# One user at a time for a PSUM bank in the list that orders a three-layer kernel

## The chip, the cores and the metric

The kernel runs on one core of a Trainium2 chip. The metric is the device time of one execution in microseconds (us), the median of three runs. TensorE (PE) multiplies and writes to PSUM, which has eight banks of 512 words per partition. VectorE (DVE) and ScalarE (ACT) read PSUM and SBUF, GpSimd (POOL) works in SBUF, SyncE (SP) issues DMAs.

## The reference

Three layers follow each other; `N` is 2304 tokens, `D` 512.

```
attention, 4 x 8 heads, 576 positions, head size 64: scores under a window mask
    (32 back, or 128 back in steps of 4), softmax, times v
x  = rows of the attention's output, normed by their root mean square, times rms_g
x  = (silu(x @ w_gate) * (x @ w_val)) @ w_out                    # d_ff = 1536
P  = exp(x @ w_gate2 - max); 8 times: rows, then columns of P scaled to sums
out = sum over 8 experts e of P[:, e] * (relu(x @ w1[e]) @ w2[e])  # F = 1024 each
```

## The kernel before

**Precision.** Each fp32 operand is split into an upper part in a rounded format and the remainder; a product takes three passes (upper by upper, upper by lower, lower by upper, `PASSES`). Every tensor that goes into a product is therefore made twice: a copy (`upper`, mostly ScalarE) and a subtraction (`lower`, VectorE or GpSimd).

**Stages.** Up to about 566 us the attention of 20 tiles and the gated layer run, in six blocks of 384 tokens, while the layer's weights are converted and sums of the experts' weights are prepared in DRAM. Then the experts run: three groups of 768 tokens, and in each 16 halves of an expert, so 48 units. A unit `u` is a first block product (`gemm1_ops`, L1123) and a second (`gemm2_ops`, L1283), each done by a scheme with seven products instead of eight (`STEPS`, L1089). The second of unit `u-1` is interleaved with the first of unit `u`. In group 0 the second weights are split on the core and stored; in groups 1 and 2 they are loaded split.

**Banks.** The seven steps of a unit accumulate in three chains, `CHAIN = "acababa"`: chain a holds steps 0, 2, 4 and 6, b steps 3 and 5, c step 1. In the first product a step is two products `q` of six matmuls with 384 columns, one bank each. In the second a step is three products `jj` of six matmuls with 256 columns: `jj` 0 and 1 share a bank, `jj` 2 has one alone (`jj // 2`, L1304). After each step VectorE adds each `jj`, scaled by `P`, to the output in SBUF (`acc`, L1395). The first product's banks are read by ScalarE and VectorE: `copied` (L1212), `added` (L1222), the two parts of h (`halves_of`, L1133, lines 1140 to 1151), `kept` (L1225), and after step 6 the four steps of L1245 and L1121. One tile of two banks (`pair`) serves chain a of even units and chains c and b of odd units; the other chains take single banks from a pool of six.

**The list.** Nothing runs by a loop on the chip. Each operation is an `Op` (L84): engine, a cost, what it reads and writes (keys), which slot it takes and frees. `Plan.add` (L106) makes dependences from the keys: a reader waits for the last writer, a writer for the readers as well; two readers of one key don't wait for each other. `Plan.run` (L122) plays the operations through a model of the engines: at each moment, each free engine starts the ready operation of the lowest rank. The order of the starts is the order in which instructions are emitted, so each engine's queue is fixed by it. Ranks of the first stages are by name (`RANK`, L34), and which engine takes a piece is in `PICK` (L64); those of the units are `at(u, s) = 1000 + 14 u + 2 s` (L1097), plus 1 for the second product. Semaphores are put in afterwards by the layer below, from the tiles and banks that instructions really touch, not from the keys. So the list sets the order on each engine, and where its idea of a wait is wrong, an engine stands at an instruction that the list thought ready.

**Keys before.** A bank's key of the first product is `("bank", u, chain, q)`; the parts of h and `kept` read it. In the second product the key is `("y", u, chain, jj)`, so the two `jj` of one bank are independent in the list. Weights of unit `u+1` are split at rank `at(u + 1, j) - 6`, behind gates on products of unit `u` (L1717, L1730).

Of the kernel before, what the change touches and what calls it, by code (L numbers as in the profile page):

```python
# [19 lines left out]
P = 128  # L20
# [50 lines left out]
    "lower c2o": "DVE", "scaled 0": "ACT", "scaled 1": "ACT", "scaled 10": "ACT", "scaled 11": "DVE",  # L71
    "scaled 12": "ACT", "scaled 2": "ACT", "scaled 6": "DVE", "scaled 7": "DVE", "scaled 8": "DVE",
# [11 lines left out]
class Op:  # L84

    def __init__(self, eng, cost, emit, reads=(), writes=(), take=(), free=(), table=None, size=0, pick=None,
                 beside=None):
        self.beside = beside
        if pick:
            self.name, self.costs = pick  # L90
            eng = PICK.get(self.name, eng)
            cost = self.costs[eng]
        self.eng, self.cost, self.emit, self.reads, self.writes = eng, cost, emit, reads, writes
        self.take, self.free, self.table, self.size = take, free, table, size
        self.rank, self.after, self.end, self.got = None, [], None, None


class Plan:

    HOP, EXTRA, LOAD, LATENCY, RATE, BESIDE = 0.1, 0.08, 1.3, 2.0, 360.0, 1.35  # L100

    def __init__(self, slots):
        self.ops, self.slots = [], {tag: list(names) for tag, names in slots.items()}
        self.writer, self.readers = {}, {}
# [17 lines left out]
    def run(self):  # L122
# [12 lines left out]
        while len(order) < len(self.ops):  # L135
# [12 lines left out]
            for i, (_, o) in enumerate(ready):  # L148
                if free[o.eng] > now or o.take and not any(self.slots[tag] for tag in o.take):
                    continue  # L150
                if o.take:
                    tag = next(tag for tag in o.take if self.slots[tag])
                    o.got = (tag, self.slots[tag].pop(0))
                span = o.cost * ((o.beside or self.BESIDE) if o.eng == "DVE" and free.get("POOL", 0.0) > now else 1.0)
                if o.table and o.table != table:
                    span, table = span + self.LOAD, o.table
                free[o.eng] = now + span if span else now + 0.01
                heappush(events, free[o.eng])
                if o.size:
                    link = max(link, now + span) + o.size / self.RATE  # L160
                    o.end = link + self.LATENCY
                else:
                    o.end = now + span + self.EXTRA
                for owner in o.free:
                    heappush(back, (o.end + self.HOP, len(order), owner.got if isinstance(owner, Op) else owner))
                    heappush(events, o.end + self.HOP)
                order.append((now, o))
                started.append(i)
                for u in users[o]:
                    needs[u] -= 1  # L170
                    if not needs[u]:
                        at = max(d.end + (0.0 if d.eng == u.eng else self.HOP) for d in u.after)
                        heappush(coming, (at, place[u], u))
                        heappush(events, at)
            for i in reversed(started):
                del ready[i]
        for _, o in order:
            o.emit()
# [4 lines left out]
def attention_moe_kernel(  # L183
# [81 lines left out]
    def att_ops(n, blk, c0, bufs, wide=False, last=(), held=()):  # L265
# [169 lines left out]
        for h in range(2):  # L435
            @op("ACT", 0.33, [("XT", n)], [("hi", n, h)])
# [4 lines left out]
            @op("DVE", 0.4, [("XT", n), ("hi", n, h), ("lo", n, 0)], [("lo", n, h)], free=[back] if h else [])  # L441
# [681 lines left out]
    def gemm1_ops(u):  # L1123
# [9 lines left out]
        def halves_of(s, m, q, key, src, relu, eng):  # L1133
            x = {}

# [8 lines left out]
            def lower():  # L1144
# [9 lines left out]
                "ACT", 0.41, upper, [key] + ([("hu", u, m, 0)] if q else []), [("hu", u, m, q)],  # L1154
                take=("xn", "h", "h2") if q == 0 else (),
            )
            if q == 0:
                h_owner[u, m] = x["up"]
            x["lo"] = Op(
                eng, 0.475, lower, [key, ("hu", u, m, q)], [("hh", u, m, q)],  # L1160
# [3 lines left out]
            add(s, x["up"])  # L1164
            return add(s, x["lo"])
# [663 lines left out]
```

## Time and profile before

| | us |
|---|---|
| median of 3 runs (2214.47 to 2222.55) | 2215.64 |
| the profiled execution, own time | 2215.74 |
| its span, first to last instruction | 2213.7 |
| TensorE busy | 2052.2 |
| TensorE granted clock, mean share of full | 0.98 |

In the profile, "idle before" is what an engine stood before an instruction, and the releaser named with it is what ended the wait. `ya`, `yb`, `yc` are the banks of the second product's chains, `pa`, `pb`, `pc` those of the first; `p`, `pq`, `u`, `r` are copies in SBUF; `h_a` and `h_s` are parts of h, `w_a`, `w_s`, `w_t`, `w_b` split weights. "x6" is six matmuls merged to one row.

### The profile page before, as it was taken

To read this page: it belongs to the slowest core of one execution; us is meant where nothing else is said; L and a number is where in the kernel's file an instruction comes from. 1 tells how busy PE (TensorE), PEld (TensorE's weight loads), DVE (VectorE), ACT (ScalarE), POOL (GpSimd) and SP (SyncE) were. 2 spreads that over 40 slices of the span, in tenths; PEclk is the share of its full clock that TensorE was granted. 3 is DMA by queue.
4 is the path that set the end of the run, shared out by engine and by line. 5 is a ranking of instruction groups with operands and counts; after the bars stand their busy time and mean duration, and the time that the engine had idled before them with its cause. 6 is when DMAs were issued, how large, how long until landed. Compare 5 with 4: busy or idle time off the path is not lost.

```text
span 2213.7 us, 40898 instructions
## 1 busy us (share of the span) xinstructions
PE 2052.2 (93%) x15654; PEld 1987.2 (90%) x15654; DVE 1456.0 (66%) x2906; ACT 1093.4 (49%) x2298; POOL 1047.6 (47%) x975
## 2 busy tenths in 40 slices
PE   6999999999899999989999989899899999999998
PEld 5999999999888888988998988899899899999998
DVE  7886545453686878768656666666665666666665
ACT  7744524332556556556554444444445544444442
POOL 1311454561466767567654443444444444435441
PEclk9999999999999999999999999999999999999999
DMA  7513788884555777777875555665576554554561
GB/s 282 185 51 109 260 277 277 280 273 157 186 211 210 263 278 257 252 260 253 316 259 187 184 181 160 201 212 186 176 254 218 167 199 161 167 180 157 184 191 47
DMA packets 210164, 459.84 MB, mean 208 GB/s; under 512 B 16560, under 2 KB 59440, under 8 KB 209968
## 3 DMA queue, kind: packets, MB, share of 16 engines
q1 hardware_dynamic: 209072, 456.44, 60.8%
q8 instruction: 123, 2.02, 0.4%
q10 hardware_dynamic: 896, 0.79, 0.1%
q14 instruction: 73, 0.60, 0.1%
HBM read 344.44 MB, written 112.72 MB: 207 GB/s over the span
## 4 chain that ended last, share of the span: by engine, by line
PE 59%; DVE 21%; DMA 7%; ACT 7%; POOL 3%; issue 3%; SPq 0%; DVEq 0%; ACTq 0%; POOLq 0%
PE pa L1183 12%; PE ya L1308 12%; PE pb L1183 8%; PE yb L1308 5%; PE pc L1183 4%; PE pg L707 4%; DVE acc L1395 4%; PE pv L707 4%; PE po L631 4%; PE yc L1308 3%; DMA spare<-in_w 3%; DVE h_a L1147 2%; DVE pq L1121 2%; ACT h_s L1142 2%; DVE p L1121 2%
## 5 line engine op out<-in xcount | busy, mean ns | idle before, releaser
L1395 DVE SCALAR_TENSOR_TENSOR acc<-ya,Pm,acc 128x256 f32<-128x256 f32 x510 | 242.0, 478 | 147.5 <-PE ya L1308 142.8
L1007 POOL TENSOR_TENSOR w_s<-w0s,w_s 128x512 fp32r<-128x512 f32 x192 | 253.9, 1327 | 168.8 <-ACT w_s L1003 168.4
L1007 POOL TENSOR_TENSOR w_a<-w0r,w_a 128x512 fp32r<-128x512 f32 x144 | 187.5, 1307 | 196.5 <-ACT w_a L1003 193.9
L1308 PE MATMUL ya<-w_t,h_s 128*128 128x256 f32 x1728 | 256.4, 284 | 17.6 <-DVE acc L1395 16.9
L1308 PEld LDWEIGHTS ya<-w_t,h_s 128*128 128x128 f32 x1728 | 236.9, 191 | 23.5 <-DVE acc L1395 20.4
L1151 POOL TENSOR_TENSOR h_s<-r,h_s 128x384 fp32r<-128x384 f32 x96 | 102.8, 1072 | 326.7 <-ACT h_s L1142 279.2
L1183 PE MATMUL pa<-x_t,w_s 128*128 128x384 f32 x1152 | 238.5, 342 | 2.4 <-ACT pq L1212 1.8
L1183 PEld LDWEIGHTS pa<-x_t,w_s 128*128 128x128 f32 x1152 | 194.8, 190 | 5.8 <-ACT pq L1212 2.0
L1308 PE MATMUL ya<-w_b,h_a 128*128 128x256 f32 x864 | 138.9, 300 | 46.1 <-DVE acc L1395 46.1
L1308 PEld LDWEIGHTS ya<-w_b,h_a 128*128 128x128 f32 x864 | 124.3, 203 | 54.5 <-DVE acc L1395 54.1
L707 PE MATMUL pg<-xn,w_g 128*128 128x384 f32 (+2 forms) x912 | 170.4, 335 | 0.0
L707 PE MATMUL pv<-xn,w_v 128*128 128x384 f32 (+2 forms) x912 | 167.5, 331 | 0.0
L631 PE MATMUL po<-h,w_o 128*128 128x384 f32 x864 | 161.1, 339 | 0.4 <-DVE h L738 0.4
L1003 ACT CAST w_s<-w0s 128x512 fp32r<-128x512 f32 x192 | 118.9, 625 | 82.9 <-POOL w_s L1007 35.4
L707 PEld LDWEIGHTS pg<-xn,w_g 128*128 128x128 f32 x912 | 155.8, 191 | 1.0
L707 PEld LDWEIGHTS pv<-xn,w_v 128*128 128x128 f32 x912 | 153.1, 188 | 1.4
L631 PEld LDWEIGHTS po<-h,w_o 128*128 128x128 f32 x864 | 151.8, 190 | 1.5 <-DVE h L738 0.7
L1151 POOL TENSOR_TENSOR h_s<-p,h_s 128x384 fp32r<-128x384 f32 x96 | 110.2, 1148 | 77.7 <-ACT h_s L1142 67.6
L1308 PE MATMUL yb<-w_t,h_a 128*128 128x256 f32 x864 | 128.5, 284 | 15.9 <-DVE acc L1395 12.0
L1183 PE MATMUL pc<-x_b,w_a 128*128 128x384 f32 x576 | 131.6, 368 | 12.1 <-DVE h_s L1151 11.1
L1308 PEld LDWEIGHTS yb<-w_t,h_a 128*128 128x128 f32 x864 | 117.3, 190 | 21.4 <-DVE acc L1395 16.5
L1395 DVE SCALAR_TENSOR_TENSOR acc<-yb,Pm,acc 128x256 f32<-128x256 f32 x258 | 122.8, 477 | 15.3 <-PE yb L1308 15.1
(215 smaller groups left out, 4582.8 us busy)
## 6 DMA issues: line engine op xcount, KB each, us to landing
w_t<-split SPq DMA_DIRECT2D x128, 512.0 KB, 3.6
w0r<-in_w SPq DMA_DIRECT2D x96, 512.0 KB, 5.8
w0s<-sums SPq DMA_DIRECT2D x96, 512.0 KB, 6.0
w_b<-split SPq DMA_DIRECT2D x96, 512.0 KB, 4.5
split<-w_t SPq DMA_DIRECT2D x64, 512.0 KB, 2.8
split<-w_b SPq DMA_DIRECT2D x48, 512.0 KB, 4.5
spare<-in_w SPq DMA_DIRECT2D x42, 512.0 KB, 5.0
sums<-spare SPq DMA_DIRECT2D x42, 512.0 KB, 4.1
```

What stands on the lines that cost most here:

```text
L631: nc.tensor.matmul(x[dc], lhsT=weights["o", f][:, a, dc * P : dc * P + P], rhs=hs[blk, f][:, bb, :n], start=k == 0, stop=k == 11,)
L707: nc.tensor.matmul(ps, lhsT=weights[nm, kt, fg][:, a, fo * P : fo * P + P], rhs=xns[blk][kt // 2][:, kt % 2, bb, c0:c1], start=k == 0, sto ...
L1003: nc.scalar.copy(w1s[u, m][:, :, 0, :], q[m])
L1007: engines[x["lo"].eng].tensor_tensor(out=v[:, :, 1, :], in0=q[m], in1=v[:, :, 0, :].bitcast(F32), op=ALU.subtract)
L1121: nc.vector.scalar_tensor_tensor(out=out, in0=x, scalar=0.0, in1=y, op0=ALU.max, op1=op)
L1142: nc.scalar.copy(hh[u, m][:, q, 0, :], src())
L1147: nc.vector.scalar_tensor_tensor(out=lo, in0=src(), scalar=0.0, in1=hi.bitcast(F32), op0=ALU.max, op1=ALU.subtract)
L1151: engines[x["lo"].eng].tensor_tensor(out=lo, in0=src(), in1=hi.bitcast(F32), op=ALU.subtract)
L1183: nc.tensor.matmul(banks[chain, q], lhsT=w1s[u, a][:, kt, hl, q * P : q * P + P], rhs=xc[g, b, kt][:, xl, :TH], start=fresh and k == 0, st ...
L1308: nc.tensor.matmul(ps, lhsT=hh[u, a][:, q, hl, jj * P : jj * P + P], rhs=w2s[u, b][:, q, wl, :], start=fresh and k == 0 and jj != 1, stop= ...
L1395: nc.vector.scalar_tensor_tensor(out=dst, in0=ps(), scalar=scale(), in1=dst, op0=ALU.mult, op1=ALU.add)
```

## The change

- **Bank keys.** Operations that read a bank of the first product now write its key, so in the list they follow each other (`halves_of`: `alone`; `kept`; two of the last steps), and `kept` is put between the two parts of h. In the attention the two upper parts now come first and the two lower ones write the bank's key.
- **One operation for a shared bank.** `jj` 0 and 1 of a second product are one operation of twelve matmuls with one key; `jj` 2 stays alone.
- **The model's clockwork.** Latency 0.12 and 0.09 us instead of 0.1 and 0.08, 0.2 behind TensorE; an operation that follows one on its own engine starts at its end; slots of single banks (and of h and xn) come back in a queue that is shared, in the order in which they were freed. Products of the routing get 0.8 us of slack.
- **Weights earlier.** Rank `- 12` instead of `- 6`; the gate of the second weights one step earlier for odd `j`.
- **RANK and PICK** are replaced: other ranks for loads, conversions, attention tiles and blocks of the first stages, other engines for some of the pieces (not shown).

```diff
-    HOP, EXTRA, LOAD, LATENCY, RATE, BESIDE = 0.1, 0.08, 1.3, 2.0, 360.0, 1.35
+    HOP, EXTRA, LOAD, LATENCY, RATE, BESIDE = 0.12, 0.09, 1.3, 2.0, 360.0, 1.35
+    PE_EXTRA = 0.2
...
+    def slot(self, o, now):
+
+        for tag in o.take:
+            if self.slots[tag]:
+                queue = self.queues.get(self.shared.get(tag, tag))
+                if queue is None or queue and queue[0] <= now:
+                    return tag
...
-                        at = max(d.end + (0.0 if d.eng == u.eng else self.HOP) for d in u.after)
+                        at = max(d.done if d.eng == u.eng and not d.size else d.end + self.HOP for d in u.after) + u.slack
...
-            @op("ACT", 0.33, [("XT", n)], [("hi", n, h)])
+            @op("ACT", 0.33, [], [("XT", n), ("hi", n, h)])
             def upper(h=h):
...
-            @op("DVE", 0.4, [("XT", n), ("hi", n, h), ("lo", n, 0)], [("lo", n, h)], free=[back] if h else [])
+        for h in range(2):
+            @op("DVE", 0.4, [("hi", n, h)], [("XT", n), ("lo", n, h)], free=[back] if h else [])
             def lower(h=h):
...
+            alone = [key] if key[0] == "bank" else []
...
-                "ACT", 0.41, upper, [key] + ([("hu", u, m, 0)] if q else []), [("hu", u, m, q)],
+                "ACT", 0.41, upper, [key] + ([("hu", u, m, 0)] if q else []), [*alone, ("hu", u, m, q)],
...
-                eng, 0.475, lower, [key, ("hu", u, m, q)], [("hh", u, m, q)],
+                eng, 0.475, lower, [key, ("hu", u, m, q)], [*alone, ("hh", u, m, q)],
...
             add(s, x["up"])
+            if between:
+                add(s, between)
             return add(s, x["lo"])
...
-                    low = halves_of(s, m, q, key, ps, True, "DVE")
-                    keep = add(s, Op("ACT", 0.372, kept, [key], [(tag, u, q)]))
+                    keep = Op("ACT", 0.372, kept, [], [key, (tag, u, q)])
+                    low = halves_of(s, m, q, key, ps, True, "DVE", keep)
...
-            for jj in range(3):
-                key = ("y", u, chain, jj)
+            for y, some in enumerate(((0, 1), (2,))):
+                key = ("y", u, chain, y)
...
-                    "PE", 6 * 0.1203, product, [("hh", u, a, 0), ("hh", u, a, 1), ("w2", u, b)], [key],
-                    take=ANY if fresh and jj != 1 else (), free=[h_owner[u, a]] if jj == 2 else [],
+                    "PE", len(some) * 6 * 0.1203, product, [("hh", u, a, 0), ("hh", u, a, 1), ("w2", u, b)], [key],
+                    take=ANY if fresh else (), free=[h_owner[u, a]] if y else [],
...
             for jj in range(3):
-                key = ("y", u, chain, jj)
+                key = ("y", u, chain, jj // 2)
...
-        })
+        }, {"mm": "b", "o": "b", "single": "b", "xn": "h"}, ("m", "m2"))
...
-                        plan.add(gated(three[:1], u, (3 + j) // 2), at(u + 1, j) - 6)
-                        plan.add(three[1:], at(u + 1, j) - 6)
+                        plan.add(gated(three[:1], u, (2 + j) // 2), at(u + 1, j) - 12)
+                        plan.add(three[1:], at(u + 1, j) - 12)
...
-                    plan.add(gated(ops[2 * j : 2 * j + 1], u, (2 + j) // 2), at(u + 1, j) - 6)
-                    plan.add(ops[2 * j + 1 : 2 * j + 2], at(u + 1, j) - 6)
+                    plan.add(gated(ops[2 * j : 2 * j + 1], u, (2 + j) // 2), at(u + 1, j) - 12)
+                    plan.add(ops[2 * j + 1 : 2 * j + 2], at(u + 1, j) - 12)
```

## Rows read from the trace of the kernel before

**Rows 1.** The page, busy time of each engine.
```profile
PE 2052.2 (93%) x15654; PEld 1987.2 (90%) x15654; DVE 1456.0 (66%) x2906; ACT 1093.4 (49%) x2298; POOL 1047.6 (47%) x975
```

**Rows 2.** Busy time by stretch: stretch, length, PE, PEld, DVE, ACT, POOL; clock, DMA.
```profile
0.00:54.00 54.00, 32.20 (x827) 27.89 (x827) 42.84 (x95) 39.18 (x83) 5.49 (x12) 1.00 0.78 287
...
600.00:1118.00 518.00, 474.46 (x3219) 458.46 (x3218) 394.13 (x767) 312.24 (x659) 347.01 (x280) 0.99 0.73 260
1118.00:2190.00 1072.00, 994.40 (x6657) 968.12 (x6656) 680.25 (x1368) 503.74 (x1068) 476.19 (x404) 0.97 0.56 184
```

**Rows 3.** Who waited, TensorE, 600 us to the end: total us, times, longest.
```profile
PE ya L1308 <- DVE acc L1395: 63.0, 28, 3.0
PE yb L1308 <- DVE acc L1395: 13.1, 16, 2.3
PE pc L1183 <- DVE h_s L1151: 11.1, 7, 1.9
PE pa L1183 <- ACT p L1212: 9.7, 11, 1.7
PE pb L1183 <- DVE u L1239: 8.9, 14, 1.9
```

**Rows 4.** Timeline, one turn of units: start us, us, engine, line, operation [idle before].
```profile
1417.75 0.88 PE L1308 MATMUL ya<-w_b,h_a 128*128 128x256 f32 x6
...
1418.47 0.88 PE L1308 MATMUL yc<-w_b,h_a 128*128 128x256 f32 x6
...
1420.92 0.47 DVE L1395 SCALAR_TENSOR_TENSOR acc<-ya,Pm,acc 128x256 f32<-128x256 f32 x1
...
1421.77 0.47 DVE L1395 SCALAR_TENSOR_TENSOR acc<-ya,Pm,acc 128x256 f32<-128x256 f32 x1
...
1422.30 0.98 PE L1308 MATMUL ya<-w_b,h_a 128*128 128x256 f32 x6 [2.95 <-DVE acc L1395]
```

**Rows 5.** Timeline of TensorE: three of the stalls that come again.
```profile
1213.61 1.65 PE L1308 MATMUL ya<-w_b,h_a 128*128 128x256 f32 x6 [2.96 <-DVE acc L1395]
...
1572.90 0.98 PE L1308 MATMUL ya<-w_t,h_s 128*128 128x256 f32 x6 [2.32 <-DVE acc L1395]
...
2162.02 1.65 PE L1308 MATMUL ya<-w_b,h_a 128*128 128x256 f32 x6 [2.96 <-DVE acc L1395]
```

**Rows 6.** Timeline of TensorE at a steady place: what a product takes.
```profile
1426.86 1.21 PE L1183 MATMUL pa<-x_t,w_s 128*128 128x384 f32 x6
1427.90 0.87 PE L1308 MATMUL yc<-w_b,h_a 128*128 128x256 f32 x6
1428.61 0.69 PE L1183 MATMUL pa<-x_t,w_s 128*128 128x384 f32 x3
```

**Rows 7.** Timeline of ScalarE: the first copy of three units that follow each other.
```profile
1889.08 0.47 ACT L1212 COPY p<-pa 128x384 f32<-128x384 f32 x1
...
1923.53 0.48 ACT L1212 COPY p<-pa 128x384 f32<-128x384 f32 x1 [0.65 <-PE pa L1183]
...
1955.73 0.47 ACT L1212 COPY p<-pa 128x384 f32<-128x384 f32 x1
```

**Rows 8.** Two stretches of 10 us: length, PE busy, granted clock, DMA share, GB/s.
```profile
1140.00:1150.00 10.00, 8.16 (x59) 1.00 0.61 185
...
1960.00:1970.00 10.00, 9.19 (x45) 0.66 0.18 54
```

**Rows 9.** Timeline of TensorE just behind a long stall.
```profile
1894.98 1.92 PE L1183 MATMUL pc<-x_b,w_a 128*128 128x384 f32 x6
1896.70 1.48 PE L1308 MATMUL ya<-w_b,h_a 128*128 128x256 f32 x6
1897.98 1.51 PE L1183 MATMUL pc<-x_b,w_a 128*128 128x384 f32 x6
```

**Rows 10.** Who waited, whole run: the remainder behind the second copy.
```profile
DVE h_a L1147 <- ACT pq L1225: 51.4, 61, 2.1
```

**Rows 11.** The page, the costliest group on VectorE.
```profile
L1395 DVE SCALAR_TENSOR_TENSOR acc<-ya,Pm,acc 128x256 f32<-128x256 f32 x510 | 242.0, 478 | 147.5 <-PE ya L1308 142.8
```

More of the change, by code (lines that the diff above doesn't have):

```diff
@@ L34 @@
 RANK = {
[26 rows of a table removed]
[26 rows of a table added]
 }
 PICK = {
[6 rows of a table removed]
-    "lower c2o": "DVE", "scaled 0": "ACT", "scaled 1": "ACT", "scaled 10": "ACT", "scaled 11": "DVE",
-    "scaled 12": "ACT", "scaled 2": "ACT", "scaled 6": "DVE", "scaled 7": "DVE", "scaled 8": "DVE",
[8 rows of a table removed]
[7 rows of a table added]
+    "scaled 0": "ACT", "scaled 1": "ACT", "scaled 10": "ACT", "scaled 11": "ACT", "scaled 12": "ACT",
+    "scaled 16": "DVE", "scaled 2": "ACT", "scaled 6": "DVE", "scaled 7": "ACT", "scaled 8": "ACT",
+    "split 1": "DVE", "taken 0 0": "DVE", "taken 1 0": "ACT", "upper c0a 0": "ACT", "upper c0a 1": "POOL",
[7 rows of a table added]
 }
@@ L86, in __init__ @@
     def __init__(self, eng, cost, emit, reads=(), writes=(), take=(), free=(), table=None, size=0, pick=None,
-                 beside=None):
-        self.beside = beside
+                 beside=None, slack=0.0):
+        self.beside, self.slack = beside, slack
         if pick:
@@ L94, in __init__ @@
         self.take, self.free, self.table, self.size = take, free, table, size
-        self.rank, self.after, self.end, self.got = None, [], None, None
+        self.rank, self.after, self.end, self.done, self.got = None, [], None, None, None
 class Plan:
-    HOP, EXTRA, LOAD, LATENCY, RATE, BESIDE = 0.1, 0.08, 1.3, 2.0, 360.0, 1.35
-    def __init__(self, slots):
+    HOP, EXTRA, LOAD, LATENCY, RATE, BESIDE = 0.12, 0.09, 1.3, 2.0, 360.0, 1.35
+    PE_EXTRA = 0.2
+    def __init__(self, slots, shared, named):
         self.ops, self.slots = [], {tag: list(names) for tag, names in slots.items()}
+        self.shared, self.named = shared, named
+        self.queues = {}
+        for tag, names in self.slots.items():
+            if tag not in named:
+                pool = shared.get(tag, tag)
+                self.queues[pool] = self.queues.get(pool, []) + [0.0] * len(names)
         self.writer, self.readers = {}, {}
@@ L120, in add, with order @@
             self.ops.append(o)
-    def run(self):
+    def slot(self, o, now):
[4 more added lines that the diff above has]
+                    return tag
+    def order(self):
         place = {o: (RANK.get(o.rank[0], o.rank[0]), o.rank[1]) for o in self.ops}
@@ L148, in run @@
             for i, (_, o) in enumerate(ready):
-                if free[o.eng] > now or o.take and not any(self.slots[tag] for tag in o.take):
+                if free[o.eng] > now:
                     continue
                 if o.take:
-                    tag = next(tag for tag in o.take if self.slots[tag])
+                    tag = self.slot(o, now)
+                    if tag is None:
+                        continue
                     o.got = (tag, self.slots[tag].pop(0))
+                    if tag not in self.named:
+                        self.queues[self.shared.get(tag, tag)].pop(0)
                 span = o.cost * ((o.beside or self.BESIDE) if o.eng == "DVE" and free.get("POOL", 0.0) > now else 1.0)
@@ L156, in run @@
                     span, table = span + self.LOAD, o.table
-                free[o.eng] = now + span if span else now + 0.01
+                free[o.eng] = now + span if span else now + 0.001
                 heappush(events, free[o.eng])
+                o.done = now + span
                 if o.size:
@@ L162, in run @@
                 else:
-                    o.end = now + span + self.EXTRA
+                    extra = 0.0 if o.eng == "NONE" else self.PE_EXTRA if o.eng == "PE" else self.EXTRA
+                    o.end = now + span + extra
                 for owner in o.free:
-                    heappush(back, (o.end + self.HOP, len(order), owner.got if isinstance(owner, Op) else owner))
-                    heappush(events, o.end + self.HOP)
+                    tag, name = owner.got if isinstance(owner, Op) else owner
+                    at = o.end + self.HOP
+                    heappush(back, (at, len(order), (tag, name)))
+                    heappush(events, at)
+                    if tag not in self.named:
+                        self.queues[self.shared.get(tag, tag)].append(at)
                 order.append((now, o))
@@ L176, in run @@
                 del ready[i]
+        return order
+    def run(self):
+        order = self.order()
         for _, o in order:
@@ L1131, in add, with halves_of @@
             return o
-        def halves_of(s, m, q, key, src, relu, eng):
+        def halves_of(s, m, q, key, src, relu, eng, between=None):
             x = {}
+            alone = [key] if key[0] == "bank" else []
             def upper():
@@ L1260, in gemm1_ops @@
                     add(s, Op("ACT", 0.41, clipped, [], [key]))
-                    hold["r", q] = add(s, Op("DVE", 0.465, step_r, [("p1", u, q), key, "right"], [("r", u, q)], take=("r",), beside=1.0))
+                    hold["r", q] = add(s, Op("DVE", 0.465, step_r, [("p1", u, q), "right"], [key, ("r", u, q)], take=("r",), beside=1.0))
                     add(s, Op("DVE", 0.465, step_s1, [("u4", u, q)], [key], free=[hold["u4", q]], beside=1.0))
-                    add(s, Op("DVE", 0.465, step_p1, [key], [("p1", u, q)], beside=1.0))
+                    add(s, Op("DVE", 0.465, step_p1, [], [key, ("p1", u, q)], beside=1.0))
                     add(s, Op("DVE", 0.465, step_pq, [("p1", u, q)], [("pq", u, q)], beside=1.7))
@@ L1297, in gemm2_ops, with product @@
             row, col = ((0, 0), (0, 0), (1, 0), (1, 1), (1, 1), (1, 0), (0, 1))[s]
-            for jj in range(3):
-                key = ("y", u, chain, jj)
-                def product(s=s, a=a, b=b, chain=chain, fresh=fresh, jj=jj):
-                    if fresh and jj != 1:
-                        banks[chain, jj // 2] = bank(f"y{chain}_{u}_{jj // 2}")
-                    ps = banks[chain, jj // 2][:, 256 * (jj % 2) : 256 * (jj % 2) + 256]
-                    k = 0
-                    for q in range(2):
-                        for hl, wl in PASSES:
-                            nc.tensor.matmul(
-                                ps,
-                                lhsT=hh[u, a][:, q, hl, jj * P : jj * P + P],
-                                rhs=w2s[u, b][:, q, wl, :],
-                                start=fresh and k == 0 and jj != 1,
-                                stop=k == 5,
-                                skip_group_check=True,
-                            )
-                            k += 1
+            for y, some in enumerate(((0, 1), (2,))):
+                key = ("y", u, chain, y)
+                def product(s=s, a=a, b=b, chain=chain, fresh=fresh, y=y, some=some):
+                    if fresh:
+                        banks[chain, y] = bank(f"y{chain}_{u}_{y}")
+                    for jj in some:
+                        ps = banks[chain, y][:, 256 * (jj % 2) : 256 * (jj % 2) + 256]
+                        k = 0
+                        for q in range(2):
+                            for hl, wl in PASSES:
+                                nc.tensor.matmul(
+                                    ps,
+                                    lhsT=hh[u, a][:, q, hl, jj * P : jj * P + P],
+                                    rhs=w2s[u, b][:, q, wl, :],
+                                    start=fresh and k == 0 and jj != 1,
+                                    stop=k == 5,
+                                    skip_group_check=True,
+                                )
+                                k += 1
@@ L1318, in gemm2_ops @@
                 o = Op(
-                    "PE", 6 * 0.1203, product, [("hh", u, a, 0), ("hh", u, a, 1), ("w2", u, b)], [key],
-                    take=ANY if fresh and jj != 1 else (), free=[h_owner[u, a]] if jj == 2 else [],
-                )
-                if jj:
-                    o.after.append(products[u, "y", s, jj - 1])
-                if fresh and jj != 1:
-                    hold[chain, jj // 2] = o
-                products[u, "y", s, jj] = add(s, o)
-                if jj == 2:
+                    "PE", len(some) * 6 * 0.1203, product, [("hh", u, a, 0), ("hh", u, a, 1), ("w2", u, b)], [key],
@@ L1328, in gemm2_ops @@
+                    take=ANY if fresh else (), free=[h_owner[u, a]] if y else [],
+                )
+                if y:
+                    o.after.append(products[u, "y", s, 0])
+                if fresh:
+                    hold[chain, y] = o
+                products[u, "y", s, y] = add(s, o)
+                if y:
                     add(s, close([o] + ([stores[u, b]] if (u, b) in stores else []), [w_owner[1, u, b]]))
             for jj in range(3):
-                key = ("y", u, chain, jj)
+                key = ("y", u, chain, jj // 2)
@@ L1421, in put @@
             def put(fn):
-                ops.append(Op(eng, cost, fn, reads, writes, take, free, table))
+                ops.append(Op(eng, cost, fn, reads, writes, take, free, table, slack=0.8 if eng == "PE" else 0.0))
                 return ops[-1]
```

80 rows, old and new, of tables (PICK, RANK) are left out of this document.

## Prediction

> **What bounds the kernel now.** I read the page's busy times first. The reader is to see TensorE at 2052.2 of 2213.7 us [rows 1], 93 per cent, the others at 66 per cent or less: TensorE is the bound, and only what makes it stand or slows it counts. The stretches say where it stands [rows 2]: 21.8 us of the first 54, when weights and attention tiles have only begun to come, little more until 566, then 518.00 - 474.46 = 43.5 us from 600 to 1118 (group 0) and 1072.00 - 994.40 = 77.6 from 1118 to 2190. So 121.1 us of standing lie among the units. In the same two stretches the granted clock is 0.99 and 0.97, which is 0.01 x 518 + 0.03 x 1072 = 37.3 us of clock lost.
>
> The waits name what ended the standing [rows 3]: 63.0 + 13.1 = 76.1 us are a second product that waits for `acc`, the rest are a dozen small causes, all on banks of the first product. The timeline shows one such wait [rows 4]. `ya` of `jj` 0 starts at 1417.75, `yc` at 1418.47, and then TensorE stands 2.95 us until 1422.30, when `ya` of `jj` 1 starts, just behind the `acc` of 1421.77. That `acc` reads `jj` 0. The two halves don't share a word, they share a bank: the semaphores keep them apart, the list of before thought them free of each other, and so put the product where TensorE must stand at it. It comes again: 14 stalls of 2.95 to 2.96 us from 1213 to 2162, one for two units, and six of 2.31 or 2.32, the last at 1572.90 [rows 5]. 14 x 2.96 = 41.4 and 6 x 2.31 = 13.9 leave 20.8 of the 76.1.
>
> The floor comes from rows at a steady place [rows 6]: six matmuls of 384 columns take 1.04 us until the next product starts, six of 256 take 0.71. A unit has 14 and 21 of them: 14 x 1.04 + 21 x 0.71 = 29.5 us, and two units 58.9. Two units take 1955.73 - 1889.08 = 66.65 us [rows 7]; the 7.7 us above the floor are standing and clock.
>
> The clock: in 10 us with 8.16 busy, so 1.84 of standing, it stayed at 1.00; in the 10 us behind a stall of 2.96 it was 0.66, so some time was spent at the lower of the two levels, 1.2 instead of 2.4 GHz [rows 8]. What that costs is in the products behind the stall [rows 9]: 1.92, 1.48 and 1.51 us against 1.21, 0.87 and 1.21 [rows 6], 1.62 us together. 20 stalls of over 2 us times 1.62 are 32.4 of the 37.3.
>
> **The change part by part.** *One operation for `jj` 0 and 1.* No instruction is added or taken away; twelve matmuls stand where six stood. (a) At the 14 stalls TensorE then has `jj` 1 of `ya` and of `yc` to do, 2 x 0.71 = 1.42 us, before it needs another bank. 14 x 1.42 = 19.9 us come back. (b) The other 1.54 us of each I take as half gained, because the list now sees the wait and may put a product of the first kind or an `acc` ahead; 14 x 0.77 = 10.8. Bounds: 0, if VectorE is what is late and all banks are taken, and 21.6. (c) The six stalls of 2.31 are the same pattern at step 2, with other work in hand: 13.9 gone. (d) Of the 20.8 us of other waits for `acc`, two thirds, 13.9; bounds 0 and 20.8. What it costs: the `acc` of `jj` 0 now starts one product later, 0.71 us. It is covered as long as VectorE, busy 680.25 of 1072 us [rows 2], catches up before chain a comes round two steps later; if the cover fails, rival 4 is the price.
>
> The page "PSUM — Partial Sum Buffer" of the Trainium skill, section "PSUM bank collisions raise a hardware error", says that any two of TensorE, ScalarE and VectorE on one bank and the same partitions at once are an error, reads against reads and disjoint columns included, so that they have to be kept apart by bank. The trace agrees with its 2.95 us at 1422.30. Read against this change, the rule says that the wait can't be removed, only turned round: all 7 x 48 pairs of halves now hold their first `acc` back by 0.71 us, 239 us of VectorE's lateness in all, and the time would be 2216 + 239 less the gains if all of it came onto TensorE's path; I count none of it, on VectorE's share.
>
> *Bank keys of the first product.* The remainder of h waits for the copy beside it, a read behind a read, 51.4 us in 61 waits [rows 10], which the list did not know. That moves nothing by itself: the real wait was there. What is gained is that TensorE's order allows for it. 121.1 - 76.1 = 45.0 us of standing are of this kind (`pc` behind `h_s`, `pa` behind `p`, `pb` behind `u`, [rows 3]); (e) I take a third, 15.0, bounds 0 and 45.0, the low side because the longest of them, `pc` behind `h_s`, waits for the pair of banks itself, which the old list knew too. The latencies, the shared queue of slots and the slack of the routing products have the same answer and are in this third.
>
> *Clock.* (f) With no stall over 2 us left most of the loss goes; two thirds of 37.3, 24.9 us. Bounds 0 and 37.3.
>
> *Weights earlier.* The same casts and subtractions, put ahead of other work of ScalarE and GpSimd, and in group 0 the stores on SyncE with them. No wait of TensorE among the units names a weight or a DMA, so being earlier gains nothing. It can cost: a cast ahead of `copied` or `kept` holds a bank longer. The nearest row is `pa` behind `p`, 9.7 us [rows 3]; bounds -9.7 and +9.7, value 0, since a third of it is already in (e).
>
> *RANK and PICK.* The same work in another order until 566 us. There are 21.8 us of standing in the first 54 [rows 2] to win, and an order that starts the dense products later loses as much: bounds -22 and +22, value 0, for nothing in the trace says which.
>
> Sum: 19.9 + 10.8 + 13.9 + 13.9 + 15.0 + 24.9 = 98.4 us. The profiled execution took 2215.74, 0.1 over the median of the runs, so 2215.7 - 98.4 = 2117.3; I say 2117.
>
> **The rivals.** *1, the forecast*, some 40 per cent of the standing left: 2117, own range 2085 to 2150.
>
> *2, nearly all goes.* The list's new idea of a bank is right everywhere and other products fill each hole. 121.1 + 37.3 = 158.4 us; at 85 per cent, 134.6: 2081. For it: the stalls repeat to 0.01 us, so they come from the order alone. Against it: around a turn VectorE gets to the last `acc` of the old unit only at 1420.92 [rows 4], and banks are the limit there.
>
> *3, the stall changes its name.* At the turn VectorE is late, not the order: TensorE does 1.42 us more, then stands for as long at the next fresh bank, because the `acc` come later by as much. Then (a), (b), (e) and (f) are nothing, (c) and (d) stay: 27.8 us, 2188. For it: the `acc` of 1421.77 comes 3 us after its product's end. Against it: VectorE does in that time steps that could come after.
>
> *4, slower.* The doubled product holds the first `acc` back 0.71 us, VectorE's queue at a turn outlasts TensorE's work in hand, and the stall, which now comes at 14 of 47 turns, comes at 16 more. Each costs 2.96 + 1.62 = 4.58 us, 73 in all, less the 27.8 of (c) and (d): 2215.7 + 45.5 = 2261. It decides from the point where VectorE's backlog at a turn exceeds two products of the first and three of the second kind, 2 x 1.04 + 3 x 0.71 = 4.2 us. Against it: an `acc` is 0.48 us [rows 11], three are 1.4, and step 2 comes that much later only in the unit's middle.
>
> *5, the list hardly moves.* Semaphores already kept the banks apart; the order, fixed by ranks, comes out nearly the same, and what the first stages win or lose is under 11 us: 2216.
>
> **How the numbers follow.** Chances: forecast 0.48, rival 2 0.22, rival 3 0.15, rival 4 0.08, rival 5 0.07. The range 2060 to 2205 holds the first three and leaves out rival 4, most of rival 5 and a rest of rival 2 whose first stages win 22 us as well. A measurement of this kernel can tell some 0.5 per cent, 11 us, from no change. Faster by more than that: 0.48 + 0.22 + 0.14 of rival 3 = 0.84. Within it: 0.01 of rival 3 and 0.07 of rival 5, 0.08. Slower: 0.08.
>
> **What would show it.** In the changed kernel's profile the twelve matmuls of `ya` stand as one row, no second product waits for an `acc` of its own bank's other half, and the waits for `acc` fall from 76 to under 30 us. (a) to (c): no stall of TensorE over 2 us after 1200. (e): waits on `pc`, `pa`, `pb` of 30 us. (f): granted clock 0.99 over the span, no 10 us under 0.80 after 1200. Two units take 62 to 63 us in group 2. Rival 3 shows as stalls of 1.5 to 3 us at the turns named `pc` or a fresh `ya`; rival 4 as stalls at odd and even turns. The first stages: the units start at 566 plus or minus 22. I am wrong in the mechanism if the waits for `acc` stay over 50 us, and in the sum if the units start much later than now.

## The result, and the profile after

The changed kernel takes 2124.94 us (median of 4 runs, 2117.82 to 2131.09), the kernel before 2215.05 beside it: ratio 0.9599, interval 0.9537 to 0.9661. The profiled execution after took 2117.82, its span is 2116.0, so 97.7 us are gone from the span. All numbers below are of the profiled executions unless a ratio stands there.

Busy time on the page of the changed kernel, to lay beside [rows 1]:

```profile
PE 2008.1 (95%) x15654; PEld 1970.1 (93%) x15654; DVE 1457.0 (69%) x2892; ACT 1082.1 (51%) x2310; POOL 1041.3 (49%) x975
```

TensorE is still the bound. Its busy time fell by 44.1 us though it does the same 15654 matmuls. Where the 97.7 us came from is told by ScalarE's first copies of units 0, 16, 32 and 47 (start, length), first of the kernel before, then of the changed one:

```profile
570.69 0.47 ACT L1212 COPY p<-pa 128x384 f32<-128x384 f32 x1
...
1110.45 0.48 ACT L1212 COPY p<-pa 128x384 f32<-128x384 f32 x1
...
1658.34 0.48 ACT L1212 COPY p<-pa 128x384 f32<-128x384 f32 x1 [0.65 <-PE pa L1183]
...
2156.93 0.47 ACT L1212 COPY p<-pa 128x384 f32<-128x384 f32 x1
```
```profile
563.36 0.47 ACT L1246 COPY p<-pa 128x384 f32<-128x384 f32 x1
...
1091.75 0.85 ACT L1246 COPY p<-pa 128x384 f32<-128x384 f32 x2
...
1596.08 0.85 ACT L1246 COPY p<-pa 128x384 f32<-128x384 f32 x2
...
2066.73 0.85 ACT L1246 COPY p<-pa 128x384 f32<-128x384 f32 x2
```

The first stages gave 7.3 us, group 0 gave 11.4 (539.8 to 528.4), group 1 43.6 (547.9 to 504.3), group 2 up to its last unit 27.9 (498.6 to 470.7), and the rest 7.5.

The stretches after, as in [rows 2] (length, TensorE busy, granted clock, DMA share, GB/s):

```profile
0.00:54.00 54.00, 29.28 (x853) 1.00 0.76 277
...
600.00:1092.00 492.00, 459.86 (x3128) 0.98 0.73 261
1092.00:2092.00 1000.00, 962.59 (x6674) 0.99 0.62 199
```

The waits of TensorE from 590 on, as in [rows 3] (total, times, longest; five of fifteen rows):

```profile
PE pc L1217 <- DVE h_s L1183: 33.7, 17, 2.1
PE pc L1217 <- DVE acc L1430: 11.0, 18, 1.9
PE yc L1343 <- DVE acc L1430: 8.9, 5, 2.1
PE pb L1217 <- DVE u L1273: 7.4, 6, 2.2
...
PE yb L1343 <- DVE acc L1430: 0.2, 1, 0.2
```

No `ya` waits for VectorE's `acc` any more, and `yb` does for 0.2 us: the two rows that held 76.1 us are gone. In their place `pc`, the new unit's first product in the pair of banks, waits for `h_s`, the last reader of the pair: 33.7 us, before 11.1. All rows together are 73.3 us, before 121.1.

TensorE's timeline at a turn of the changed kernel (start, us; [idle before <-releaser]):

```profile
1869.33 2.25 PE L1217 MATMUL pa<-x_b,w_s 128*128 128x384 f32 x12
1871.41 2.31 PE L1343 MATMUL ya<-w_b,h_s 128*128 128x256 f32 x18
1873.56 2.25 PE L1217 MATMUL pa<-x_b,w_a 128*128 128x384 f32 x12
1875.65 2.31 PE L1343 MATMUL ya<-w_b,h_a 128*128 128x256 f32 x18
1880.00 2.35 PE L1217 MATMUL pc<-x_b,w_a 128*128 128x384 f32 x12 [2.05 <-DVE h_s L1183]
1882.19 2.31 PE L1343 MATMUL yc<-w_b,h_a 128*128 128x256 f32 x18
```

Two things are to be seen. Each row is a whole step: 12 matmuls of the first product, then 18 of the second, where before halves alternated (six and six, [rows 6]). And at 1880.00 TensorE has stood 2.05 us. This comes at every second turn, 16 times from 1124.08 to 2068.44; the turns between have 0.15 to 0.47. VectorE at the same turn shows what the pair waited for:

```profile
1870.38 0.86 DVE L1430 SCALAR_TENSOR_TENSOR acc<-yb,Pm,acc 128x256 f32<-128x256 f32 x2
...
1872.12 0.56 DVE L1152 SCALAR_TENSOR_TENSOR r<-p,pa 128x384 f32<-128x384 f32 x1 [0.87 <-ACT pa L1279]
...
1876.67 1.17 DVE L1152 SCALAR_TENSOR_TENSOR pq<-pq,p 128x384 f32<-128x384 f32 x1
1877.77 1.25 DVE L1430 SCALAR_TENSOR_TENSOR acc<-ya,Pm,acc 128x256 f32<-128x256 f32 x3
1878.94 1.00 DVE L1183 TENSOR_TENSOR h_s<-pa,h_s 128x384 fp32r<-128x384 f32 x2
```

All eight steps of L1152 run first, from 1872.12 to 1877.8, then three `acc`, then the two remainders that free the pair.

### The profile page after: what moved, and what is told of

Read it like the earlier page. It is cut to its first block, busy times and chain, and to the rows that moved or that the text cites. A ratio compares the mean times of both kernels' runs of the same rounds, so it can differ in the third digit from the quotient of the medians.

```text
span 2116.0 us, 40970 instructions
## 1 busy us (share of the span) xinstructions
PE 2008.1 (95%) x15654; PEld 1970.1 (93%) x15654; DVE 1457.0 (69%) x2892; ACT 1082.1 (51%) x2310; POOL 1041.3 (49%) x975
## 4 chain that ended last, share of the span: by engine, by line
PE 67%; DVE 24%; ACT 5%; issue 2%; DMA 1%; POOL 0%; SPq 0%; DVEq 0%; ACTq 0%; POOLq 0%
PE pa L1217 11%; PE ya L1343 9%; PE pb L1217 8%; PE yb L1343 7%; PE pv L738 6%; PE pg L738 6%; PE po L662 6%; PE pc L1217 6%; PE yc L1343 5%; DVE pq L1152 4%; DVE acc L1430 3%; DVE h_a L1179 2%; DVE p L1152 2%; DVE pa L1152 2%; DVE r L1152 2%
## 5 line engine op out<-in xcount | busy, mean ns | idle before, releaser
L1430 DVE SCALAR_TENSOR_TENSOR acc<-ya,Pm,acc 128x256 f32<-128x256 f32 x510 | 216.6, 471 | 46.7 <-PE ya L1343 46.7
L1343 PE MATMUL ya<-w_t,h_s 128*128 128x256 f32 x1728 | 223.2, 283 | 1.3 <-ACT acc L1389 1.2
L1217 PE MATMUL pa<-x_t,w_s 128*128 128x384 f32 x1152 | 218.9, 337 | 4.5 <-ACT pq L1246 2.2
L1343 PEld LDWEIGHTS ya<-w_t,h_s 128*128 128x128 f32 x1728 | 218.8, 191 | 2.2 <-ACT acc L1389 1.5
L1430 DVE SCALAR_TENSOR_TENSOR acc<-yb,Pm,acc 128x256 f32<-128x256 f32 x258 | 111.7, 476 | 106.1 <-PE yb L1343 106.1
L1217 PE MATMUL pc<-x_b,w_a 128*128 128x384 f32 x576 | 125.6, 371 | 46.2 <-DVE h_s L1183 33.7
L1217 PEld LDWEIGHTS pc<-x_b,w_a 128*128 128x128 f32 x576 | 109.7, 208 | 53.7 <-DVE h_s L1183 37.2
L1343 PE MATMUL yc<-w_b,h_a 128*128 128x256 f32 x864 | 118.2, 292 | 12.3 <-DVE acc L1430 8.9
L1343 PEld LDWEIGHTS yc<-w_b,h_a 128*128 128x128 f32 x864 | 115.8, 200 | 13.6 <-ACT h_s L1174 12.6
L991 POOL TENSOR_TENSOR spare<-spare 128x256 f32<-128x256 f32 x126 | 96.8, 771 | 63.4 <-DMA spare<-in_w 35.0
L1172 ACT ACTIVATE h_a<-pc 128x384 fp32r<-128x384 f32 x96 | 47.6, 495 | 144.5 <-DVE pc L1256 140.8
```

The source lines that it names most:

```text
L991: engines[o.eng].tensor_tensor(out=out_, in0=in0, in1=in1, op=alu)
L1172: nc.scalar.activation(hh[u, m][:, q, 0, :], src(), AF.Relu)
L1217: nc.tensor.matmul(banks[chain, q], lhsT=w1s[u, a][:, kt, hl, q * P : q * P + P], rhs=xc[g, b, kt][:, xl, :TH], start=fresh and k == 0, st ...
L1343: nc.tensor.matmul(ps, lhsT=hh[u, a][:, q, hl, jj * P : jj * P + P], rhs=w2s[u, b][:, q, wl, :], start=fresh and k == 0 and jj != 1, stop= ...
L1430: nc.vector.scalar_tensor_tensor(out=dst, in0=ps(), scalar=scale(), in1=dst, op0=ALU.mult, op1=ALU.add)
```

## The experiments

Each ran in three rounds beside the kernel before; a ratio is to that kernel. Of each edit only the main lines are shown. Line numbers of an experiment may differ by a few from those above.

**a1, the merge alone** (kernel before, with `jj` 0 and 1 as one operation and one key):

```diff
-            for jj in range(3):
-                key = ("y", u, chain, jj)
+            for y, some in enumerate(((0, 1), (2,))):
+                key = ("y", u, chain, y)
```

> The kernel before with one part of the change alone: jj 0 and 1 of a second product are one operation with one key. Theory 1 (the stall between the halves of a bank is what the change removed): 2125 to 2150 us, waits of TensorE for acc under 30 us. Theory 2 (the rule that an operation starts right at the end of its predecessor on the same engine regroups TensorE's order into whole steps, and that alone does it): more than half of the 90 us stays away, 2175 or more. Theory 3 (the first stages' new ranks are most of it): 2205 or more.

2124.89 us, 0.9601 (0.9572 to 0.963): all of the change's gain. The waits of `ya` and `yb` for `acc` (here L1396) fall from 76.1 to 2.7 us. What stands is the first product's, in halves of a step:

```profile
PE pb L1183 <- DVE h_a L1147: 17.7, 11, 1.8
PE pc L1183 <- DVE h_a L1147: 15.5, 18, 0.9
PE pc L1183 <- DVE h_s L1151: 14.1, 21, 1.2
```

All its waits are 77.7 us (73.3 in the change). So the other waits rose here too, from 45.0 to 75.0: of the 73 us that the cure took from one wait, 30 came back under other names.

**a2, the rule alone** (kernel before, with only the model's rule for an operation behind one of its own engine; three separate `jj` and their three keys stay):

```diff
-  at = max(d.end + (0.0 if d.eng == u.eng else self.HOP) for d in u.after)
+  at = max(d.done if d.eng == u.eng and not d.size else d.end + self.HOP for d in u.after)
```

> The kernel before with the rule for operations on the same engine alone (start at the end of the predecessor, not 0.08 us behind it). Theory 1: 2190 or more, the stalls at jj 1 stay. Theory 2: 2120 to 2150, the three jj stand together in TensorE's order, two units take 62 to 64 us in group 2. Theory 3: 2205 or more.

2110.03 us, 0.9538 (0.9511 to 0.9564). The first theory fell: one line of the model removes the stall without the merge, and no `ya` or `yb` waits for VectorE's `acc`. The second theory's order came, its time was better than its range. By the code of the list, with the old rule the next `jj` became ready 0.08 us behind the end of the one before, so at that moment the list found only the other product ready and took it; with the new one the next `jj` is ready at once, has the lowest rank and follows. TensorE then runs in whole steps, and the two `jj` of a bank stand together anyway. The price is the wait of the pair, here as a total and at one turn:

```profile
PE pc L1184 <- DVE h_s L1152: 40.5, 23, 5.8
...
1868.52 2.35 PE L1184 MATMUL pc<-x_b,w_a 128*128 128x384 f32 x12 [2.04 <-DVE h_s L1152]
```

**a3, the change without the merge:**

```diff
-            for y, some in enumerate(((0, 1), (2,))):
-                key = ("y", u, chain, y)
+            for jj in range(3):
+                key = ("y", u, chain, jj)
```

> The changed kernel with jj 0, 1 and 2 as three operations with three keys again. Theory 1: 2170 or more, stalls of 2 to 3 us behind acc come back. Theory 2: 2117 to 2140.

2107.49 us, 0.9521 (0.9489 to 0.9553), with the same whole steps and the same 33.7 us of `pc` behind `h_s`. Beside the rule the merge is not needed. It may even cost: the waits of `pc` and `yc` for `acc` (here L1429, in the change L1430) are 4.4 us here and 19.9 in the change, most of them in group 0, and all waits are 67.9 and 73.3. The times differ by some 17 us, but the two intervals touch, so by time the two can't be told apart. The time is below theory 2's range as well.

**a4, the change with the old rule:**

```diff
-  at = max(d.done if d.eng == u.eng and not d.size else d.end + self.HOP for d in u.after) + u.slack
+  at = max(d.end + (0.0 if d.eng == u.eng else self.HOP) for d in u.after) + u.slack
```

> The changed kernel with the old rule for operations on the same engine (0.09 us behind TensorE's others, 0.2 behind TensorE itself). Theory 1: 2117 to 2140, since the merge is there. Theory 2: 2150 or more, single products interleaved again and small bubbles between them.

2089.38 us, 0.9444 (0.9414 to 0.9473), faster than the change and clear of its interval, some 34 us. The halves came back as theory 2 said, but both theories' times were too long. This is the version that beats both kernels. Its three longest waits:

```profile
PE pb L1217 <- ACT h_a L1172: 12.4, 17, 1.0
PE pc L1217 <- DVE h_s L1183: 11.5, 21, 0.7
PE pa L1217 <- ACT p L1246: 7.9, 8, 1.3
```

The same stretch of both (busy of PE, PEld, DVE, ACT, POOL; clock), first of a4, then of the change:

```profile
1092.00:2037.00 945.00, 924.00 (x6455) 914.13 (x6454) 636.02 (x1323) 487.12 (x1042) 465.85 (x398) 1.00 0.63 207
```
```profile
1092.00:2037.00 945.00, 909.64 (x6303) 902.43 (x6304) 639.04 (x1299) 472.99 (x1023) 449.70 (x392) 0.99 0.64 204
```

a4 stands 21.0 of 945 us at clock 1.00, the change 35.4 at 0.99. The same turn in a4, TensorE and VectorE, shows how it goes:

```profile
1846.46 1.21 PE L1217 MATMUL pa<-x_b,w_s 128*128 128x384 f32 x6
...
1850.70 0.48 DVE L1430 SCALAR_TENSOR_TENSOR acc<-ya,Pm,acc 128x256 f32<-128x256 f32 x1
...
1851.55 0.48 DVE L1430 SCALAR_TENSOR_TENSOR acc<-ya,Pm,acc 128x256 f32<-128x256 f32 x1
...
1853.22 0.48 DVE L1430 SCALAR_TENSOR_TENSOR acc<-ya,Pm,acc 128x256 f32<-128x256 f32 x1
...
1854.96 1.60 PE L1343 MATMUL yc<-w_b,h_a 128*128 128x256 f32 x12
...
1857.14 1.31 PE L1217 MATMUL pc<-x_b,w_a 128*128 128x384 f32 x6 [0.58 <-DVE h_s L1183]
```

From step 6's first product to the pair's release it takes 10.68 us here (1846.46 to 1857.14) and 10.67 in the change (1869.33 to 1880.00): the pair is not free earlier. But VectorE puts the old unit's `acc` between its steps, a single bank is free by 1854.96, and TensorE does twelve matmuls of `yc` there; it then stands 0.58 us and not 2.05. That this makes the whole gain is argued from this turn, not shown.

**b2, the first product's keys alone** (kernel before with `halves_of`, `kept` and the last steps of the change):

```diff
-  "ACT", 0.41, upper, [key] + ([("hu", u, m, 0)] if q else []), [("hu", u, m, q)],
+  "ACT", 0.41, upper, [key] + ([("hu", u, m, 0)] if q else []), [*alone, ("hu", u, m, q)],
```

> The kernel before with the keys of the first product alone (parts of h, kept and two steps write the bank's key, kept between the parts). Theory 1 (the wait between the halves of a second product's bank is what cost): those waits stay, 2190 to 2215 us. Rival (what counts is that the list knows every bank of the first product): 2160 or less.

2174.43 us, 0.9822 (0.9783 to 0.9862), between what the theories gave: some 40 us by itself, though `ya` still waits 48.6 and `yb` 14.9 us for `acc` (63.5 of 76.1). All waits from 600 on fall to 91.6 us, the others from 45.0 to 28.1, and the clock rises from 0.980 to 0.987. That part doesn't add to the others.

**b4, the pair always for chains c and b** (the change; chain a of every unit in single banks):

```diff
-            whole = (u % 2 == 0) == (chain == "a")
+            whole = chain != "a"
```

> The changed kernel with another use of the pair of banks: chains c and b of every unit have it, chain a never. Theory P (pc stands 2.05 us at every second turn because the pair is still held by chain a's tail): no stall over 1 us at pc after 1200, two units take 59.5 to 61 us, 2075 to 2095 us. Rival V (VectorE is late at the turn, whichever bank is asked for): the stall comes at yc or pc at every turn, 2115 or more.

2102.28 us, 0.9497 (0.9461 to 0.9533). `pc` no longer waits in the units, as theory P said, but its time did not come, nor the rival's: the standing only moved:

```profile
PE ya L1338 <- DVE acc L1425: 53.7, 39, 2.0
...
1861.60 2.42 PE L1338 MATMUL ya<-w_b,h_a 128*128 128x256 f32 x18 [1.54 <-DVE acc L1425]
...
1855.00:1865.00 10.00, 8.46 (x60) 1.00 0.49 169
```

Of these 39 waits 23 are of 1.54 or 1.55 us and 6 of 1.15 or 1.16, at nearly every turn from 1111 us on. All waits are 71.7 us, nearly as much as in the change (73.3). What is won is the clock: 0.997 over the span against 0.988. No stall of over 2 us comes between 621 and 2079 us.

**c1, the old rule for the units' TensorE products only, and d2, for all of the units' operations** (the change; `late_` is rank 1000 or more, in c1 for TensorE alone; the line is c1's, in d2 an operation also starts without `HOP` behind a DMA of its own engine):

```diff
-  at = max(d.done if d.eng == u.eng and not d.size else d.end + self.HOP for d in u.after) + u.slack
+  at = max((d.end if late_ else d.done) if d.eng == u.eng and not d.size else d.end + self.HOP for d in u.after) + u.slack
```

> The changed kernel; products of the units alone keep the old rule (a product is ready 0.2 us behind the product it follows), all other operations keep the new one. Theory G (with the old rule the halves of a step stand apart in TensorE's order, so chain a's tail begins half a step earlier and the pair comes back in time): two units take 61 to 62 us in group 2, the units start at 563 as in the changed kernel, 2075 to 2085 us. Rival (the gain of the old rule lies in other engines' order): 2105 or more.

> The changed kernel with the old rule for all operations of the units and the new rule for the first stages. Theory G (the units of a4 and the first stages of the changed kernel add): units start at 563 to 566, 2078 to 2084 us. Rival (the start of the units is not given by the rule, or the list at the border moves as well): 2088 or more.

c1: 2101.47 us, 0.9488 (0.9458 to 0.9519), between the theories' times. The wait went as theory G said: `pc` behind `h_s` is 1.7 us, in the change 33.7. So the rule for TensorE's products alone takes that stall away. d2: 2092.38, 0.9455 (0.942 to 0.9489), like a4 and in its rival's range. By the medians two thirds of a4's gain come with the rule for TensorE's products; the rest would come with the other engines', but c1 and d2 are not clear of each other. The new rule's earlier start of the units, 565.7 against 572.6 us, did not add up in d2's time.

**d1 and d3, a4 and d2 with b4's pair:**

```diff
-            whole = (u % 2 == 0) == (chain == "a")
+            whole = chain != "a"
```

> The run a4_old_same_engine (2089 us) with the pair of banks for chains c and b of every unit. Theory G with P (halves apart and the pair free at the turn are two gains): pc no longer waits for h_s, 2075 to 2085 us. Rival V (VectorE's backlog is the limit, the wait only goes to ya as in b4): 2085 to 2105.

> d2 with the pair of banks for chains c and b of every unit. Theory G with P: 2068 to 2080 us, the fastest. Rival V: not under d2, 2080 to 2100.

2117.65 us, 0.9563 (0.9534 to 0.9592), and 2114.28, 0.9547 (0.9519 to 0.9576): the pair that gained in whole steps costs 28 and 22 us in halves. Waits of d1:

```profile
PE pb L1217 <- ACT h_a L1172: 27.0, 39, 1.7
PE pc L1217 <- ACT h_a L1172: 21.0, 31, 2.1
```

Chains b and c now sit in the pair in each unit, and these rows name ScalarE's casts of it (`h_a`) as late for the next step; why they are late is not shown. Both theories of both runs gave less time than was measured.

**b1, RANK and PICK of before in the change, and b3, the weights' ranks and gate of before:**

```diff
-    "att8": 1.0, "raw2": 6.87, "raw11": 8.23, "out00": 8.28, "v8": 9.78,
...
+    "raw0": 0, "raw13": 1, "h11": 2, "att1": 3, "raw24": 4,
```

```diff
-  plan.add(gated(three[:1], u, (2 + j) // 2), at(u + 1, j) - 12)
+  plan.add(gated(three[:1], u, (3 + j) // 2), at(u + 1, j) - 6)
```

> The changed kernel with RANK and PICK of the kernel before. Theory 1 (the new ranks are worth what the start of the units moved by, some 7 us): units start at 566 to 575, 2125 to 2140 us. Rival (the first stages matter more, since the old ranks were found for the old model): 2150 or more.

> The changed kernel with the weights' ranks and gates of before (6 ahead instead of 12, the gate of the second weights one step later for odd j). Theory 1 (weights earlier gain nothing, since no wait of TensorE names one): 2115 to 2135 us. Rival (they were late at places, or the casts' new place sets the turn): 2150 or more, or 2105 or less.

2129.0 us, 0.9604 (0.9567 to 0.9642), and 2125.09, 0.9597 (0.9568 to 0.9626), each as its theory 1 said: neither part can be told from none in the time; a gain of 7 us would be too small to tell. In b1 the units began at 567.93 us, in the change at 563.36, before at 570.69.

## Why the prediction was right, and where not

It said 2117, with a sum of 98.4 us gone; 97.7 went from the span. The median is 8 us above the forecast, the profiled execution (2117.82) at it. That the two sums agree to 0.7 us is luck: the first cause was right, but other terms were wrong and made each other good. The terms, each against what the rows give:

- **Waits for `acc`, (a) to (d), 58.5 of 76.1.** Rows of after that name `acc` at a product (of L1430) hold 20.1 us (11.0 of them first products, `pc`), so 56.0 went. Right in size. The cause was right, as a1 shows, which does only this. But in the change the rule for operations of one engine would have done it alone (a2, a3), and the prediction does not weigh that rule at all: its "in this third" names the latencies, the queue and the slack.
- **First-product waits, (e), +15.0 of 45.0.** Wrong, in sign too: other waits are 53.2 us now, 8.2 more. The keys alone do what was said of them (b2: 16.9 less). The step that failed is to take this term as free of the others: with the stall behind `acc` cured, TensorE stands at the next thing that is late, also in a1 (75.0 of other waits). In the change this is `pc` behind `h_s`, which grew from 11.1 to 33.7, 16 stalls of 2.04 to 2.06. It is rival 3's mechanism at half the turns, made by the new rule: with the old one it is 11.5 (a4). For the same reason "no stall over 2 us after 1200" was missed, narrowly, and "waits on `pc`, `pa`, `pb` of 30 us" widely: they are 59.2. A small misreading besides: not all of the 45.0 is on banks of the first product, 4.7 are second products, mostly `yb` behind another line of `acc`.
- **Clock, (f), 24.9 of 37.3.** Clock lost over the span: 2213.7 x 0.020 = 44.3 before, 2116.0 x 0.012 = 25.4 after, so 18.9 came back. The working charged 1.62 us to each of 20 stalls, but behind five of them the clock did not fall: it was 1.00 in the 4 us from the row behind the stall, for example from 1422.30. The part that did not come back is told below.
- **RANK and PICK, weights: 0.** Standing outside the rows of waits fell by 5.8, nearly all of it before 590 us (36.0 to 30.1), and the units began 7.3 earlier, within the 22 given. b1 and b3 agree with the zeros, but can't tell them from gains of this size.
- **Not in the sum: 25.2 us.** Busy time fell 44.1 us, of which the clock explains 18.9. What is left is, for the most part, small waits that a row of six matmuls swallows. In the kernel before:

```profile
1940.74 0.87 PE L1308 MATMUL yb<-w_t,h_s 128*128 128x256 f32 x6
1941.47 1.31 PE L1183 MATMUL pa<-x_t,w_s 128*128 128x384 f32 x6
1942.62 0.87 PE L1308 MATMUL yb<-w_t,h_s 128*128 128x256 f32 x6
```

From 1941.47 to the next product it takes 1.15 us at full clock where 1.04 is the floor [rows 6]. In the change a whole step is at its floor (18 x 0.71 / 6 = 2.13 and 2 x 1.04 = 2.08), 2.15 us and 2.09:

```profile
1894.89 2.31 PE L1343 MATMUL ya<-w_t,h_s 128*128 128x256 f32 x18
1897.04 2.25 PE L1217 MATMUL pb<-x_t,w_a 128*128 128x384 f32 x12
1899.13 2.31 PE L1343 MATMUL yb<-w_t,h_a 128*128 128x256 f32 x18
```

The prediction had put the whole 7.7 us per two units above the floor on standing and clock; about 2 were of this kind. So the total was right because (e), 23.2 us short, (f), 6.0 short, and (a) to (d), 2.5 short, were made good by these 25.2 us and by the 5.8 above. Two units take 62.3 us, as foretold (63.8 where the clock fell).

These small waits can be added up over 600 to 2060 us: of each row of such a product its distance to the next row, less idle time and floor, where that is under 0.3 us. They are 48.6 us before and 23.1 in the change. The other kernels in whole steps (a2, a3, b4) have 21.9 to 23.1, those in halves that are cured of the stall (a1, a4, c1, d1 to d3) 30.4 to 33.6, and b2, which is not cured, 52.4. So whole steps are worth some 9 of the 25 us; the larger part goes in halves as well, and why is not shown.

The 239 us that the prediction weighed, for holding back the `acc` of `jj` 0, came at most in small part. No row of `ya` waits for VectorE's `acc`; `pc` and `yc` do for 19.9 us, and 15.5 of these go when the merge is taken out (a3). VectorE is busy 1457.0 of 2116.0 us.

What stays open: a version that ranks the last `acc` of the old unit ahead of the eight steps, in whole steps, was not tried.

## What to carry to other kernels

When an order is fixed by a model, the model should guard what the semaphores guard, here the bank and not the half of it; else an engine can be sent to stand at an instruction that the list thought ready. In a2 and a3 the list did not guard it, and a rule of readiness happened to give the same order. Two cures of one stall don't add (by their ratios the merge brings 88 us, the rule 102, the whole change 89), and one of them may open a new stall, so take a change apart on the chip before keeping it whole. A readiness rule that differs by only 0.08 us (a2) or 0.2 us behind TensorE (a4) changed the grain of the whole order, half steps or whole steps. Which grain is better is not general: the kernel before gained 102 us with the rule that makes whole steps, where its stall went as well, the change 34 with the one that makes halves.

## What was not expected of the hardware

The clock falls behind a stall of 2.05 us in some cases and not in others. In the change, in 7 of the 16 stalls the twelve matmuls behind it took 2.98 to 3.69 us instead of 2.35, as here, with the clock of 4 us around this stall's end and behind the one at 1880.00 (length, TensorE busy, clock). The first row is of group 0:

```profile
632.49 3.63 PE L1217 MATMUL pc<-x_b,w_a 128*128 128x384 f32 x12 [1.54 <-DVE acc L1406]
...
1816.16 3.04 PE L1217 MATMUL pc<-x_b,w_a 128*128 128x384 f32 x12 [2.05 <-DVE h_s L1183]
1819.00 3.21 PE L1343 MATMUL yc<-w_b,h_a 128*128 128x256 f32 x18
...
1816.00:1820.00 4.00, 3.84 (x17) 0.70 0.23 54
1880.00:1884.00 4.00, 4.00 (x28) 1.00 0.18 32
```

At 0.70 the engine spent part of the 4 us at the lower level, 1.2 GHz. Behind b4's 23 stalls of 1.54 or 1.55 us it never did (its eighteen matmuls took 2.40 to 2.42 us each time), nor did the clock fall in the stretch of [rows 8] with 1.84 us of standing, or in the 4 us behind it. But length alone does not decide. The 1.54 us at 632.49, behind two matmuls of 8 columns, were followed by twelve matmuls of 3.63 us and a clock of 0.59 in 4 us; in the kernel before, the clock stayed at 1.00 behind 2.95 us at 1422.30 and 2.96 at 1630.27. What decides is not shown here.

On the whole, standing in short stalls cost less: b4 stands nearly as long as the change, its profiled execution is 17.0 us shorter, and the clock, worked out as above, accounts for all of that (2116.0 x 0.012 - 2099.0 x 0.003 = 19.1).
